# Cosine attention and a leaky-ReLU feed-forward: a planned stretch in the middle of the kernel replaced by an order written out by hand

## The chip, the cores and the metric

One NeuronCore of a Trainium2 chip runs the whole program. The metric is device time in microseconds (us) of one execution. The kernel before takes 428.02 us, the median of three runs (427.03 to 428.38).

The engines are named as the profile names them: PE (TensorE, matmuls; PEld are its weight loads), DVE (VectorE), ACT (ScalarE), POOL (GpSimd) and SP (SyncE, which here only issues DMAs). Each engine works through its own list of instructions in the order in which the program issued them; semaphores make one engine wait for another.

## The reference, cut to what matters

```python
# attention: 8 batches, 12 heads, 448 positions, 64 wide
q_n = q / (norm(q) + 1e-06);  k_n = k / (norm(k) + 1e-06)
scores = q_n @ k_n.T / tau                      # tau = 0.1
attn = exp(scores - max) / (sum(...) + 1e-09)
x = (attn @ v), heads side by side              # 3584 tokens, 768 wide
# feed-forward
h = x @ w_in                                    # 768 -> 2048
out = maximum(0.01 * h, h) @ w_out              # 2048 -> 768
```

Since the scores are cosines divided by 0.1, the kernel leaves the maximum out and takes the exponential at once.

## The kernel before, in words

**Tiles.** The work is cut in 48 slots. Slots 0 to 11 (batches 0 and 1) each hold q and k of one pair of heads. From slot 12 on (`OLD`, line 118) an even slot holds q and the next odd slot k of two pairs at once; such two slots are a unit, and slots 12 and 13 are unit 0. An attention group j is two pairs of heads; groups 3, 4 and 5 are those of batch 1 (slots 6 and 7, 8 and 9, 10 and 11). The tokens are cut in 8 chunks for the feed-forward; chunk 0 is the first 384 tokens of batch 0, chunk 1 the 512 tokens after them (the rest of batch 0 and all of batch 1).

**What a slot goes through**, with the engine and the line:

- `load_qk` (line 128): the load, issued by SP (lines 136, 144 to 147) into one of four buffers. A load waits until `normalise` and `squares` of the slot four before are done with the buffer.
- `squares` (195): POOL multiplies the raw tile by itself (lines 201, 208). `hold` (585) is a one-element copy on POOL that makes POOL wait for a `normalise` before its next squares.
- `sums` (210): DVE adds up the squares (216, 222). `roots` (226): two small ACT instructions that turn the sums into norms (229, 230).
- `normalise` (234): three or four DVE instructions, the last of which writes the normalised bf16 tile (238, 239, 245 or 255).
- `transposes` (283): up to slot 11 seven PE transposes (269) and a DVE copy (310); from slot 12 on a DVE transpose (291) and, for odd slots, six DMAs issued by SP that lay out the tiles of the unit (300).

**Attention.** `scores` and `key_tiles` (317, 320) and, for units, `quad_tiles` (391) multiply keys with queries into two PSUM banks per tile; ACT takes the exponentials (340, 408). `attend` (681) is one group of batch 1: `totals` (358: 16 matmuls, then two ACT instructions, 362 and 363, which give the reciprocal of the sums), two `products` (368) into two banks, and two `scale` (377: DVE, line 382), which write the attended tile `xT` and free the two banks. Two slots' tiles of batch 1, ki = 3, come as one tile with the odd slot.

**Feed-forward.** `first` (470) is 6 matmuls (line 476) and one ACT instruction (485); `second` (503) is 16 matmuls (line 507) and one DVE copy (518), and at its second half an output DMA on SP (527). Chunk 0 has 16 of the first and 6 of the second: 22 feed-forward groups. `feed_groups` (546) issues the next ones. The weights of `second` come in two halves by `load_w_out` (111), issued by POOL; the second half, which the last three groups of chunk 0 use, is asked for shortly before the stretch that is changed.

**PSUM.** `banks` (78) deals out the eight banks, always the pair or the single one whose last dealing is oldest. Which bank an instruction gets, and so whom it waits for, follows from the order in which the program asks.

**What sets the order.** Batch 0 and the first half of batch 1 are written out by hand (lines 619 to 745), up to the 13th feed-forward group of chunk 0, `normalise(10)` and `squares(11)`. Behind it stands a plan: the table `opened` (752) of five stretches with the attention group and the score tiles of each, and a loop (763) that hands out eight of the nine groups of chunk 0 that are left, by weights (`ATTEND`, `BLOCK`). In each stretch the slot `ahead` goes through `sums`, `roots`, `normalise`, `transposes`, the load of the slot two on, `hold` and the `squares` of the next slot. In the loop's stretches 2 and 3 `attend` stands first, then the scores, `sums`, `roots`, the feed-forward and only then the slot's `prepare`; the DVE instructions of `scale` get their inputs late and stand in DVE's list behind whatever the program issued between. Lines 800 to 803 then issue the load of slot 18, `sums(15)`, `squares(16)` and `roots(15)`.

From line 808 on a second plan lists the visits: three quad tiles in each, the products of the groups, and as many feed-forward groups as the level of the remaining work gives. Its visit 0 begins with `normalise(15)`, makes one quad tile, then `attend(5)` (`NEWQ - 1`), two more quad tiles and the one group of chunk 0 that was held back (`held`, 836). A weight of 3000 in `side` (831) stands for that `attend`. Chunk 1's groups begin behind visit 1's quad tiles.

## Time and profile before

| what | value |
|---|---|
| median of the runs | 428.02 us (427.03 to 428.38) |
| the profiled execution, its own time | 429.49 us |
| its span, first to last instruction | 427.7 us |
| what lies around the span | 1.8 us |
| busy: PE, ACT, DVE, POOL | 412.0, 255.2, 222.3, 116.7 us |
| mean granted TensorE clock | 0.992 |

The profile is one execution. Its views are: the page (busy times, the span in 40 slices with the granted clock, the costliest groups of instructions), the stretches (busy time of each engine between two times), the waits (who waited for whom), the chain of waits that ended last, and the timeline (instructions in order of time, merged; in brackets the idle time of the engine just before, and what ended it). A row such as `L402 PE MATMUL ps<-qkT` is line 402 on PE, writing `ps` from `qkT`; `xN` merges N instructions. Times of rows are from the span's start.

### The profile page before, as it was taken

To read this page: it belongs to the slowest core of one execution; us is meant where nothing else is said; L and a number is where in the kernel's file an instruction comes from. 1 tells how busy PE (TensorE), PEld (TensorE's weight loads), DVE (VectorE), ACT (ScalarE), POOL (GpSimd) and SP (SyncE) were. 2 spreads that over 40 slices of the span, in tenths; PEclk is the share of its full clock that TensorE was granted. 3 is DMA by queue.
4 is the path that set the end of the run, shared out by engine and by line. 5 is a ranking of instruction groups with operands and counts; after the bars stand their busy time and mean duration, and the time that the engine had idled before them with its cause. 6 is when DMAs were issued, how large, how long until landed. Compare 5 with 4: busy or idle time off the path is not lost.

```text
span 427.7 us, 11313 instructions
## 1 busy us (share of the span) xinstructions
PE 412.0 (96%) x4779; PEld 213.0 (50%) x4797; DVE 222.3 (52%) x385; ACT 255.2 (60%) x430; POOL 116.7 (27%) x149
## 2 busy tenths in 40 slices
PE   7899999879999999999999999999999999999996
PEld 2334544434455555554445555554445555654463
DVE  5887867564577755756673884366521312120021
ACT  3986866457866678657883868647674444104300
POOL 3875651353233323323430433033110000000000
PEclk9999999969999999999999999999999999999999
DMA  6999998676376862774374494643441200020021
GB/s 153 188 228 225 223 226 127 162 193 166 89 150 178 186 169 75 190 169 122 90 173 132 95 234 124 130 116 127 88 87 38 77 37 4 22 87 3 2 74 74
DMA packets 41907, 53.82 MB, mean 126 GB/s; under 512 B 12545, under 2 KB 32257, under 8 KB 41857
## 3 DMA queue, kind: packets, MB, share of 16 engines
q1 hardware_dynamic: 25680, 40.88, 34.3%
q0 software_dynamic: 15488, 11.80, 19.0%
q8 instruction: 37, 0.61, 0.6%
q10 hardware_dynamic: 688, 0.43, 0.4%
q14 instruction: 14, 0.11, 0.1%
HBM read 45.61 MB, written 11.01 MB: 132 GB/s over the span
## 4 chain that ended last, share of the span: by engine, by line
PE 85%; DMA 5%; DVE 4%; ACT 2%; SPq 1%; issue 1%; POOL 1%; ACTq 0%; POOLq 0%; DVEq 0%
PE ps L507 34%; PE ps L476 31%; PE ps L427 9%; PE ps L402 7%; DMA qk_h<-in_q_dram 3%; DMA qk_h<-in_k_dram 2%; DVE qn L255 1%; PE ps L351 1%; PE ps L331 1%; SPq L300 1%; PE ps L269 1%; PE ps L578 1%; ACT pe L340 1%; DVE qn L245 1%; DVE qkT L310 0%
## 5 line engine op out<-in xcount | busy, mean ns | idle before, releaser
L507 PE MATMUL ps<-w_out_sb,hT 128*128 128x384 bf16 x896 | 154.0, 330 | 1.2 <-DVE xT L382 1.2
L476 PE MATMUL ps<-xT,w_in_sb 128*128 128x384 bf16 (+1 forms) x753 | 149.8, 352 | 0.9 <-issue 0.2
L408 ACT ACTIVATE pe<-ps 128x896 bf16<-128x896 f32 x126 | 109.0, 916 | 43.5 <-PE ps L402 43.5
L507 PEld LDWEIGHTS <-hT 128*128 128x128 bf16 x896 | 86.2, 99 | 67.6 <-issue 14.2
L476 PEld LDWEIGHTS <-w_in_sb 128*128 128x128 bf16 x768 | 73.1, 98 | 73.5 <-issue 8.4
L485 ACT ACTIVATE hT<-ps 128x384 bf16<-128x384 f32 (+1 forms) x128 | 68.1, 548 | 62.8 <-PE ps L476 62.3
L518 DVE COPY osb<-ps 128x384 f32<-128x384 f32 (+1 forms) x56 | 30.9, 552 | 111.9 <-PE ps L507 106.2
L201 POOL TENSOR_TENSOR sq<-qk_h 128x896 f32<-128x896 f32 x36 | 61.2, 1701 | 6.2 <-DMA qk_h<-in_k_dram 5.0
L587 POOL CAST seen<-qn 128x1 f32<-128x1 bf16 x46 | 8.4, 184 | 174.2 <-DVE qn L245 168.0
L245 DVE TENSOR_TENSOR qn<-qk_h,r 128x896 bf16<-128x896 f32 x36 | 42.6, 1183 | 1.2
L402 PE MATMUL ps<-qkT 64*32 64x448 bf16 x1008 | 37.1, 354 | 3.5 <-ACT pe L408 3.5
L216 DVE TENSOR_REDUCE ss<-sq 128x14 f32<-128x896 f32 x36 | 37.5, 1042 | 4.0 <-POOL sq L201 4.0
L340 ACT ACTIVATE pe<-ps 128x896 bf16<-128x896 f32 x42 | 35.9, 917 | 5.7 <-PE ps L331 5.7
L238 DVE TENSOR_REDUCE r<-norms 128x14 f32<-128x28 f32 x48 | 8.6, 179 | 46.6 <-ACT norms L230 46.2
L291 DVE STREAM_TRANSPOSE tt<-qn 128x448 f32<-128x448 f32 x36 | 29.5, 820 | 0.9
L452 DVE TENSOR_TENSOR xT<-ps,rb 128x448 bf16<-128x448 f32 x32 | 18.4, 618 | 21.9 <-PE ps L427 20.8
L229 ACT ACTIVATE ss<-ss,tiny 128x14 f32<-128x14 f32 x48 | 14.6, 305 | 22.4 <-DVE ss L216 18.1
L427 PE MATMUL ps<-pe,vq 64*32 64x448 bf16 x1008 | 27.0, 349 | 0.0
L208 POOL TENSOR_TENSOR sq<-qk_h 128x384 f32<-128x384 f32 (+1 forms) x21 | 20.8, 1005 | 16.3 <-DMA qk_h<-in_k_dram 16.2
L402 PEld LDWEIGHTS <-qkT 64*32 64x32 bf16 x1008 | 13.1, 91 | 23.9 <-issue 18.8
L427 PEld LDWEIGHTS <-vq 64*32 64x32 bf16 x1008 | 14.5, 92 | 8.0 <-issue 0.3
L255 DVE TENSOR_TENSOR qn<-qk_h,r 128x512 bf16<-128x512 f32 (+1 forms) x24 | 17.0, 748 | 0.4
(52 smaller groups left out, 215.5 us busy)
## 6 DMA issues: line engine op xcount, KB each, us to landing
qk_h<-in_q_dram SPq DMA_DIRECT2D x36, 224.0 KB, 4.6
qk_h<-in_k_dram SPq DMA_DIRECT2D x36, 224.0 KB, 4.2
out_dram<-osb SPq DMA_DIRECT2D x20, 384.0 KB, 2.6
qkT<-tt SPq DMA_DIRECT2D x72, 56.0 KB, 2.1
qkT<-tt SPq DMA_DIRECT2D x36, 112.0 KB, 2.4
vq<-in_v_dram POOLq DMA_DIRECT2D x16, 224.0 KB, 4.8
w_in_sb<-in_moe_w_in_dram POOLq DMA_DIRECT2D x4, 768.0 KB, 10.4
w_out_sb<-in_moe_w_out_dram POOLq DMA_DIRECT2D x2, 1536.0 KB, 21.1
```

What stands on the lines that cost most here:

```text
L201: gp.tensor_tensor(sq, raw[s], raw[s], op=ALU.mult)
L216: nc.vector.tensor_reduce(ss[s], sqs[s].rearrange("p (t d) -> p t d", d=D), axis=AX.X, op=ALU.add)
L245: nc.vector.tensor_tensor(qn[s].rearrange("p m d e -> p m e d"), raw[s].rearrange(f"p ({t[1:-1]} d) -> p m e d", e=n, d=D), r.rearrange(f" ...
L291: nc.vector.transpose(out=to.rearrange(("p g (c m) -> p m g c", "p g (m c) -> p m g c")[which], m=7), in_=qn[s].bitcast(F32).rearrange("p ...
L340: nc.scalar.activation(out=dst, in_=sc[:, :, :S], func=AF.Exp, scale=inv_tau)
L402: nc.tensor.matmul(out=sc[32 * strip : 32 * strip + 32, a, :S], lhsT=x[rows, c0 : c0 + 32], rhs=x[rows, 0:S], start=True, stop=True,)
L408: nc.scalar.activation(out=pq[u, i], in_=sc[:, :, :S], func=AF.Exp, scale=inv_tau)
L427: nc.tensor.matmul(out=po[32 * strip : 32 * strip + 32, w, :S], lhsT=weights, rhs=pq[us[x if two else 0], i][rows, a, :], start=(i == 0), ...
L476: nc.tensor.matmul(out=pm[:, :n], lhsT=w_in_sb[:, kt, m * 128 : (m + 1) * 128], rhs=xT[c // 2][:, kt, c0 : c0 + n], start=(kt == 0), stop= ...
L485: nc.scalar.activation(out=hT[c][:, m, :n], in_=pm[:, :n], func=AF.Prelu, alpha=0.01)
L507: nc.tensor.matmul(out=po2[:, :HALF], lhsT=hT[c][:, m, ts * 128 : (ts + 1) * 128], rhs=w_out_sb[:, m, half * HALF : (half + 1) * HALF], st ...
L518: nc.vector.tensor_copy(out=o[:, half * HALF : half * HALF + cut], in_=po2[:, :cut])
```

## The change

The planned stretches and the three lines of constants go. In their place stands one order, written out, with the same operations. What differs:

- The loads of slots 15 and 16 stand ahead of unit 0's six tile DMAs (line 300, issued with slot 13) in SP's list; before they stood behind them. Squares go two slots ahead of `normalise` (`settle`), not one.
- `sums` and `roots` of slots 13, 14 and 15 stand one stretch ahead of the `normalise` that uses them; `roots(15)` stands before `attend(5)`.
- `attend(3)` and `attend(4)`, with their `scale`, stand ahead of `normalise(12)` and `normalise(13)` in DVE's list; before they stood behind them. Score tiles 10 and 11 of the third stretch come ahead of `attend(4)`.
- `transposes(10)` has a feed-forward group ahead of it; its copy and the eviction of that group come ahead of `sums(11)`.
- All nine groups that are left of chunk 0 are issued here. Visit 0 has its `attend(5)` ahead of it, prepares slot 15 before its three quad tiles, and then issues four groups of chunk 1. Since nothing is held back any more, the second plan shifts some feed-forward groups between later visits: whole groups move by a visit, and at the end the last visit has ten groups of `first` where it had six.

```diff
@@ -41,8 +41,6 @@
-    ATTEND = 5500
-    BLOCK = 1800
@@ -743,64 +741,66 @@
     hold(qn[s + 4][:, 6, 0, 0:1])
     squares(s + 5)
-    feed_groups(0, 1)
-    opened = [
-        (None, [(2, 0), (2, 1), (2, 2)], 5),
-        (None, [(3, 0), (3, 1), (3, 2)], 6),
-        (0, [(4, 0), (4, 1), (3, 3)], 7),
-        (1, [(4, 2), (5, 0), (5, 1)], 8),
-        (None, [(5, 2), (5, 3)], None),
-    ]
-    queue = []
-    b = 1
-    queue += work[0]
-    costs = [BLOCK + (ATTEND if at is not None else 0) for at, _, _ in opened[1:] + [(2, 0, 0)]]
-    for i, (at, tiles, ahead) in enumerate(opened):
-        share = (sum(g[0] for g in queue[:-1]) + sum(costs[i:])) / (len(opened) - i) - costs[i]
-        if at is not None:
-            attend(b * NQ + at)
-        if i == 0:
-            load_v(b * NQ + 2)
-        key_tiles([(b * NPAIR + p, ki) for p, ki in tiles])
-        done = 0
-        s = b * NPAIR + ahead if ahead else NSLOT
-        sums(s)
-        roots(s)
-        if i < 2:
-            if i == 1:
-                cost, fn = queue.pop(0)
-                fn()
-                done += cost
-            transposes(NPAIR + 4 + i)
-
-        def prepare():
-            normalise(s)
-            if s >= OLD:
-                transposes(s)
-            for n in ((s + 2,), (s + 2, s + 3))[i == 3]:
-                load_qk(n)
-            hold(qn[s][:, 6, 0, 0:1])
-            squares(s + 1)
-
-        if i < 2:
-            prepare()
-        while len(queue) > 1 and (i == len(opened) - 1 or done + queue[0][0] / 2 <= share):
-            cost, fn = queue.pop(0)
-            fn()
-            done += cost
-        if i in (2, 3):
-            prepare()
-        if i == 3:
-            load_vq(0)
-    load_qk(OLD + 6)
-    sums(OLD + 3)
-    squares(OLD + 4)
-    roots(OLD + 3)
+    load_v(s // 2 + 2)
+    load_qk(s + 7)
+    squares(s + 6)
+    feed_groups(0, 1)
+    def settle(s):
+        normalise(s)
+        if s >= OLD:
+            transposes(s)
+        hold(qn[s][:, 6, 0, 0:1])
+        squares(s + 2)
+
+    scores(s + 2, (0, 1, 2))
+    feed_groups(0, 1)
+    transposes(s + 4)
+    sums(s + 5)
+    feed_groups(0, 2)
+    roots(s + 5)
+
+    scores(s + 3, (0, 1, 2))
+    load_qk(s + 8)
+    settle(s + 5)
+    feed_groups(0, 1)
+    sums(s + 6)
+    roots(s + 6)
+    transposes(s + 5)
+    attend(NQ)
+
+    scores(s + 4, (0, 1))
+    scores(s + 3, (3,))
+    load_qk(s + 9)
+    settle(s + 6)
+    sums(s + 7)
+    feed_groups(0, 1)
+    roots(s + 7)
+
+    scores(s + 4, (2,))
+    scores(s + 5, (0, 1))
+    feed_groups(0, 1)
+    attend(NQ + 1)
+    load_qk(s + 10)
+    settle(s + 7)
+    sums(s + 8)
+
+    scores(s + 5, (2, 3))
+    feed_groups(0, 1)
+    load_vq(0)
+    roots(s + 8)
+    load_qk(s + 11)
+    settle(s + 8)
+    load_qk(s + 12)
+    sums(s + 9)
+    feed_groups(0, 1)
+    roots(s + 9)
+    attend(NEWQ - 1)
+    feed_groups(0, 1)
@@ -829,16 +829,16 @@
     side = [
-        3000 if n == 0 else 0 if n not in parts or parts[n][1] is None else 7 * S
+        0 if n not in parts or parts[n][1] is None else 7 * S
         for n in range(len(visits))
     ]
-    held = [(False, g) for g in queue]
+    held = []
...
-        scaling = n == 0 or e is not None
+        scaling = e is not None
@@ -852,8 +852,6 @@
         quad_tiles(tiles[:1])
-        if n == 0:
-            attend(NEWQ - 1)
```

In the new code s is 6, so `s + 9` is slot 15.

## The prediction

> **What bounds the kernel now.** I read the page first, then the busy times by stretches, then PE's waits, then the timeline around the longest wait.

> ```profile
> PE 412.0 (96%) x4779; PEld 213.0 (50%) x4797; DVE 222.3 (52%) x385; ACT 255.2 (60%) x430; POOL 116.7 (27%) x149
> ```

> ```profile
> 58.00:95.00 37.00, 32.19 (x348) 16.20 (x348) 24.66 (x43) 19.58 (x36) 13.67 (x15) 0.91 0.85 173
> 95.00:370.00 275.00, 274.35 (x3687) 144.02 (x3699) 146.68 (x235) 182.62 (x301) 65.88 (x80) 1.00 0.48 119
> 370.00:427.70 57.70, 53.98 (x300) 29.26 (x299) 7.22 (x14) 9.87 (x17) 0.00 (x0) 1.00 0.14 48
> ```

> Behind the length stand the busy us of PE, PEld, DVE, ACT and POOL, then granted clock, DMA share and GB/s. PE bounds the kernel: from 95 to 370 us it idles 0.65 us, so there is nothing to win there, only to lose. In 58 to 95, the stretch that the change rewrites, it idles 4.8 us and its clock is 0.91. Who makes it wait:

> ```profile
> PE ps L402 <- ACT pe L408: 3.5, 1, 3.5
> PE ps L507 <- DVE xT L382: 1.2, 2, 0.8
> ```

> The timeline around the wait of 3.5 us:

> ```profile
> 75.45 3.77 SPq L300 DMA_DIRECT2D qkT<-tt  x6
> 79.34 1.16 SPq L136 DMA_DIRECT2D qk_h<-in_k_dram  x2
> 84.09 1.68 POOL L201 TENSOR_TENSOR sq<-qk_h 128x896 f32<-128x896 f32 x1 [2.98 <-DMA qk_h<-in_k_dram]
> 85.81 1.09 DVE L216 TENSOR_REDUCE ss<-sq 128x14 f32<-128x896 f32 x1 [3.37 <-POOL sq L201]
> 86.93 0.31 ACT L229 ACTIVATE ss<-ss,tiny 128x14 f32<-128x14 f32 x1 [6.20 <-DVE ss L216]
> 87.39 0.90 ACT L408 ACTIVATE pe<-ps 128x896 bf16<-128x896 f32 x1
> 88.34 0.57 PE L402 MATMUL ps<-qkT 64*32 64x448 bf16 x8 [3.48 <-ACT pe L408]
> 88.84 5.30 PE L507 MATMUL ps<-w_out_sb,hT 128*128 128x384 bf16 x16
> 94.07 0.79 PE L402 MATMUL ps<-qkT 64*32 64x448 bf16 x24
> ```

> It is one chain. SP issues the load of slot 15 only behind the six tile DMAs of unit 0, so the load starts at 79.3 and the squares at 84.1. The sums and roots follow; `roots(15)` stands in ACT's list ahead of visit 0's first exponential, which therefore starts at 87.4 although its matmuls were long done; and PE's third quad tile waits for that exponential's bank. Then 16 matmuls take 5.30 us. Why:

> ```profile
> 86.00:88.00 2.00, 0.00 (x0) 0.00 (x0) 1.32 (x3) 1.04 (x3) 0.97 (x2) 0.84 1.02 272
> 93.00:94.00 1.00, 1.00 (x4) 0.28 (x2) 0.00 (x0) 0.00 (x0) 0.00 (x0) 0.50 0.77 161
> 94.00:95.00 1.00, 0.86 (x25) 0.37 (x26) 0.78 (x3) 0.43 (x1) 0.00 (x0) 0.91 0.35 84
> ```

> The clock is granted at a half: a mean of 0.84 over 86 to 88 means the fall came near 87.4, some 2.5 us after PE stopped (88.34 less 3.48 is 84.86); 0.91 over 94 to 95 puts its return at 94.2.

> **The change part by part.** First PE's own list, to the end of visit 0's three quad tiles, where everything that the old program had done before its quad tiles of 94.07 is done too. Durations, start to start where two rows follow each other:

> ```profile
> 55.64 0.81 PE L269 MATMUL ps<-id,qn 128*128 128x128 bf16 x7 [0.89 <-DVE qn L255]
> 56.29 3.09 PE L476 MATMUL ps<-xT,w_in_sb 128*128 128x384 bf16 x18
> 61.91 0.76 PE L331 MATMUL ps<-qkT 64*64 64x448 bf16 x12
> 62.60 2.77 PE L507 MATMUL ps<-w_out_sb,hT 128*128 128x384 bf16 x16
> 69.65 2.76 PE L507 MATMUL ps<-w_out_sb,hT 128*128 128x384 bf16 x16 [0.81 <-DVE xT L382]
> 72.34 0.75 PE L351 MATMUL ps<-pe,ones 128*32 128x448 bf16 x12
> 74.73 0.76 PE L331 MATMUL ps<-qkT 64*64 64x448 bf16 x12
> ```

> A `first` group is a third of 3.09, 1.03; twelve score matmuls are 0.69 (61.91 to 62.60); a `second` group is 2.69 (69.65 to 72.34), an `attend` 2.39 (72.34 to 74.73), seven transposes about 0.6. The transposes of slot 10 end at 56.29 in both orders, since their source sets that; the change puts one `first` group into the 0.89 us in front of them. From 56.29 PE has left: two `first` 2.06, six `second` 16.14, three `attend` 7.17, score matmuls 12+12+12+8 2.53, transposes 0.6, 24 quad matmuls 0.69 (as the scores): 29.2 us, so 85.5 against 94.07, if nothing waits. These 8.6 us are the 1.0 of the moved group, the 3.48, the 0.81 and the rest of the 1.2, and 5.30 less 2.77, 2.5, for the clock, with some 0.4 of hand-overs.

> What is late next? DVE and ACT hand work to and fro, and there the new order is a chain.

> ```profile
> L216 DVE TENSOR_REDUCE ss<-sq 128x14 f32<-128x896 f32 x5 | 5.4, 1078 | 4.0 <-POOL sq L201 4.0
> L382 DVE TENSOR_TENSOR xT<-ps,rb 128x448 bf16<-128x448 f32 x6 | 3.4, 609 | 0.2 <-ACT rb L363 0.2
> L518 DVE COPY osb<-ps 128x384 f32<-128x384 f32 x6 | 3.3, 558 | 6.8 <-PE ps L507 6.8
> L291 DVE STREAM_TRANSPOSE tt<-qn 128x448 f32<-128x448 f32 x4 | 3.3, 818 | 0.1
> ```

> ```profile
> 73.34 0.54 ACT L362 ACTIVATE rb<-ps 128x448 f32<-128x448 f32 x1 [1.56 <-PE ps L351]
> 73.91 0.58 ACT L363 ACTIVATE rb<-rb 128x448 f32<-128x448 f32 x1
> 87.51 0.18 DVE L238 TENSOR_REDUCE r<-norms 128x14 f32<-128x28 f32 x1 [0.62 <-ACT norms L230]
> 88.00 1.17 DVE L245 TENSOR_TENSOR qn<-qk_h,r 128x896 bf16<-128x896 f32 x1
> ```

> Prices: `scale` twice 0.61, 1.22; `normalise` 1.66 (87.51 to 89.17), DVE transpose 0.82, sums 1.08, so 3.6 with hand-overs for "a slot"; roots 0.46 (86.93 to 87.39); the two logarithm instructions of `totals` 1.15 (73.34 to 74.49); an exponential 0.9. Now in the new lists. The first `second` group ends on PE at 61.7; its eviction 0.56, `sums(12)` 1.08 and `roots(12)` 0.46 lead to 63.9, the logarithms of `attend(3)` to 65.0, `scale(3)` to 66.3. The bank that the next `second` group gets comes from its first half, at 65.7, against PE at 65.4: a wait of 0.3 is left of the 0.81, because `scale` no longer stands behind `normalise(12)` and its transpose. On: slot 12 with `sums(13)` 69.9; `roots(13)` 70.4; three exponentials, which stand behind these roots on ACT, 73.1; logarithms 74.3; `scale(4)` 75.5; slot 13 with `sums(14)` 79.1; roots with an eviction beside them 79.7; slot 14 with `sums(15)` 83.3; `roots(15)` 83.8; logarithms of `attend(5)` 85.0; `scale(5)` 86.2, say 86.4 with hand-overs. The bank dealing gives the third quad tile of visit 0 the two banks of `attend(5)`, so PE, there at 85.6, waits 0.8 and the quad tiles end at 86.6. Squares are no part of this: the load of slot 15 now goes out when slot 11's buffer is free, near 61, and POOL has each square done a stretch before its sum.

> Next the transfers that move. The loads of 15 and 16 used to start at 79.3 and later; now they start near 61 and, behind `normalise(12)`, near 68. There the DMA queues were moving the second half of `w_out`:

> ```profile
> 53.95 1.16 POOL L113 DMA_DIRECT2D w_out_sb<-in_moe_w_out_dram  x1
> ```

> ```profile
> w_out_sb<-in_moe_w_out_dram POOLq DMA_DIRECT2D x1, 1536.0 KB, 17.5
> ...
> qkT<-tt SPq DMA_DIRECT2D x8, 56.0 KB, 2.0
> ```

> ```profile
> 69.00:70.00 1.00, 0.35 (x3) 0.21 (x3) 1.00 (x3) 1.00 (x2) 1.00 (x1) 1.00 1.40 196
> ```

> The last column of the DMA rows is the median time to landing. `w_out` landed at 53.95 plus 17.5, 71.5; the new order wants it on PE for the fourth `second` group at 74.7. The two loads are 2 x 448 KB; at the row's 196 GB/s 4.7 us. If they go wholly ahead of `w_out`, it lands at 76.2 and PE waits 1.5; if not at all, nothing. I take the first, the end that the row is nearer to, a saturated engine share (1.40). PE would then reach the third quad tile after the bank is free: the two waits don't add up, and the quad tiles end at 87.3.

> [...]

> Sum: 94.07 less 86.6 to 87.3 is 6.8 to 7.5. I take 6.9, near the `w_out` case. The profiled execution, 429.49 (span 427.7 and 1.8 around it), would become 422.6; it lies 1.5 above the median, and on the median's footing the forecast is 428.02 less 6.9, **421.1**.

> Edits at no cost, and their cover. Unit 0's tiles leave DVE near 78 and need 3.77 us on SP and about 2 to land, 83.9; their reader comes at 85: cover 1. Unit 1's tiles: `normalise(15)` follows `scale(5)`, tile DMAs from 89.5 to 93.3, landed at 95.5; the reader is the second tile of visit 2, behind two times four groups of chunk 1:

> ```profile
> 95.02 5.13 PE L476 MATMUL ps<-xT,w_in_sb 128*128 128x512 bf16 x23 [0.16 <-issue]
> ```

> 87 plus 2 x 5.35 plus 1.0 is 98.7: cover 3. The shifted groups of later visits are the same matmuls; where a chunk starts, a `second` group (2.69) less now lies between `scale` and its reader, and the last visit's end has three `first` groups less behind the last products, where chunk 6's six `second` groups remain as cover for their `scale`. I cost these at nothing, down to the 0.65 us that could be won there and up to 1 us lost.

> **The rivals.**

> *R1, the stall moves.* The DVE and ACT chain runs through `scale(5)`. If it is over 1.7 us longer than summed, the third quad tile waits more than 2.5 us and the clock falls again, another 2.5 to 2.7. For it: roots still stand in front of exponentials on ACT, now `roots(13)`, and in front of logarithms, `roots(15)`. Against: DVE was busy 24.7 of 37 us. End at 88.3 plus 2.7, 91.0: 3.1 gained, 424.9.

> [...]

> *R2, absorbed later.* PE comes 7 us earlier to the visits; slots 15 to 17 or the loads do not keep up, and it waits there. Against: a cover of 3 at unit 1. If half is given back: 424.5.

> *R3, slower: `w_out`.* If the second half lands at X, PE idles X less 74.7 and the clock falls. The quad tiles then end at 85.8 plus that plus 2.7; this equals 94.07 from X = 80.3, 8.8 us later than now. Against: the added 917 KB would have to pass at 104 GB/s. For it: 196 GB/s was the sum of all queues, and the row does not show how they share it. At X = 82: 429.7.

> *R4, it doesn't do what it says.* The load of 15 still waits, for its buffer or another queue, and the same stall stands at another place: 428.0. Against: in SP's list it now stands ahead of everything that waited.

> **How the numbers follow.** Forecast (gain 5.5 to 8.6) 0.70; R1 0.12; R2 0.09; R3 0.05; R4 0.04. The range reaches from PE alone, 8.6 gained (419.4), to R1 at 424.9; outside lie R3, R4 and the tail of R2. About 0.3%, 1.3 us, is what a measurement of this kernel can tell from no change. Faster by more than that: forecast, R1 and most of R2, 0.90; within it R4, 0.04; slower R3 and what is unseen, 0.06.

> **What would show it.** The profile after should have no wait of PE on line 408 over 1 us and a clock of 1.00 throughout; the squares of slot 15 should not wait for their load; `scale(3)` and `scale(4)` should stand ahead of the slots' `normalise`; a wait of PE at line 507 for a DMA near 75 would show `w_out`; a wait at line 402 for line 382 near 86 the chain. Chunk 1's first group should start near 87 where it started at 94.8. The forecast is wrong if PE idles over 2.5 us at one place, or if 95 to 370 loses more than 1 us.

## The result, and the profile after

| | before | after |
|---|---|---|
| median | 427.91 us (4 runs) | 421.27 us (4 runs, 421.03 to 421.61) |
| ratio | | 0.9848, 95% interval 0.983 to 0.9865 |
| profiled execution, its span | 429.49, 427.7 us | 421.03, 419.2 us |
| mean granted clock of it | 0.992 | 1.000 |

The change takes 6.6 us off the median; the forecast was 6.9. Over all the runs of this study before has a median of 428.27 (37 runs beside the experiments) and after one of 421.5 (12 runs, 421.03 to 422.37). Lines of the code after stand two lower than before: 402 is 400, 507 is 505, 382 is 380.

The page of after, PE's busy time; then its stretches, with the columns as in the prediction; then all that PE waits for:

```profile
PE 410.0 (98%) x4797; PEld 211.9 (51%) x4797; DVE 223.0 (53%) x385; ACT 254.4 (61%) x430; POOL 116.6 (28%) x149
```

```profile
58.00:95.00 37.00, 36.62 (x381) 18.51 (x381) 27.31 (x44) 23.86 (x42) 14.67 (x16) 1.00 0.92 196
95.00:370.00 275.00, 275.00 (x3713) 145.34 (x3712) 145.37 (x234) 176.76 (x292) 64.23 (x78) 1.00 0.48 117
```

```profile
PE ps L576 <- DVE pe L559: 1.6, 1, 1.6
PE ps L267 <- DVE qn L253: 1.0, 1, 1.0
PE ps L329 <- ACT pe L338: 0.8, 3, 0.3
PE ps L329 <- ACT norms L228: 0.8, 1, 0.8
PE ps L329 <- DVE qkT L308: 0.6, 2, 0.3
PE ps L505 <- DVE xT L380: 0.4, 1, 0.4
```

PE's idle time between 58 and 95 us has fallen from 4.8 to 0.4 us, and the clock there has risen from 0.91 to 1.00. The wait of 3.5 us at the quad tiles has no row any more. The one row left in the changed stretch is the last, 0.4 us for a `scale`. The work that is the same in both, from chunk 1's first group to the end, takes the same time: 419.2 less 85.5 (below) is 333.7 us, and before 427.7 less 94.8, plus the 0.7 us of the quad tiles that stood ahead of it there, is 333.6. The whole gain lies ahead of that point.

The timeline of after, by engines: SP first, then the slot of the long wait through POOL, DVE and ACT, then PE.

```profile
61.67 1.54 SPq L134 DMA_DIRECT2D qk_h<-in_k_dram  x2
67.57 1.10 SPq L134 DMA_DIRECT2D qk_h<-in_q_dram  x2
77.26 4.17 SPq L298 DMA_DIRECT2D qkT<-tt  x6
...
76.64 1.68 POOL L199 TENSOR_TENSOR sq<-qk_h 128x896 f32<-128x896 f32 x1
...
81.27 1.04 DVE L214 TENSOR_REDUCE ss<-sq 128x14 f32<-128x896 f32 x1
82.22 0.55 DVE L516 COPY osb<-ps 128x384 f32<-128x384 f32 x1
83.97 1.16 DVE L380 TENSOR_TENSOR xT<-ps,rb 128x448 bf16<-128x448 f32 x2 [1.20 <-ACT rb L361]
...
82.34 0.31 ACT L227 ACTIVATE ss<-ss,tiny 128x14 f32<-128x14 f32 x1 [3.67 <-DVE ss L214]
82.80 0.53 ACT L360 ACTIVATE rb<-ps 128x448 f32<-128x448 f32 x1
...
65.46 2.76 PE L505 MATMUL ps<-w_out_sb,hT 128*128 128x384 bf16 x16 [0.38 <-DVE xT L380]
74.44 5.37 PE L505 MATMUL ps<-w_out_sb,hT 128*128 128x384 bf16 x32
84.83 0.76 PE L400 MATMUL ps<-qkT 64*32 64x448 bf16 x24
85.53 4.71 PE L474 MATMUL ps<-xT,w_in_sb 128*128 128x512 bf16 x21
```

The load of slot 15 (the first row) goes out at 61.7 instead of 79.3, ahead of the six tile DMAs. Its squares (76.64) no longer wait for it, and its sums (81.27) stand in their turn on DVE. ACT still waits 3.67 us for those sums, with `roots(15)` at the head of its list, but now PE has nothing that needs ACT in that time. The 24 quad matmuls run in one piece at 84.8, before they were in three, and chunk 1 begins at 85.5.

The second half of `w_out` in the DMA view of after (issued at 53.69; last column the time to landing):

```profile
w_out_sb<-in_moe_w_out_dram POOLq DMA_DIRECT2D x1, 1536.0 KB, 20.7
```

It lands at 74.4, and PE takes it up at 74.44: no wait of the matmuls, and no cover left. The weight load in front of them does wait for it; PEld's row in the waits between 58 and 95 us:

```profile
PEld L505 <- DMA w_out_sb<-in_moe_w_out_dram: 0.4, 1, 0.4
```

### The profile page after: what moved, and what is told of

Read it like the earlier page. It is cut to its first block, busy times and chain, and to the rows that moved or that the text cites. A ratio compares the mean times of both kernels' runs of the same rounds, so it can differ in the third digit from the quotient of the medians.

```text
span 419.2 us, 11328 instructions
## 1 busy us (share of the span) xinstructions
PE 410.0 (98%) x4797; PEld 211.9 (51%) x4797; DVE 223.0 (53%) x385; ACT 254.4 (61%) x430; POOL 116.6 (28%) x149
## 4 chain that ended last, share of the span: by engine, by line
PE 89%; DMA 3%; DVE 3%; ACT 3%; issue 0%; SPq 0%; DVEq 0%
PE ps L505 35%; PE ps L474 33%; PE ps L425 9%; PE ps L400 7%; PE ps L349 3%; DMA qk_h<-in_q_dram 3%; DVE qn L253 2%; ACT pe L338 1%; PE ps L329 1%; PE ps L576 1%; DMA qk_h<-in_k_dram 1%; PE ps L267 1%; ACT ss L227 0%; ACT hT L483 0%; ACT norms L228 0%
## 5 line engine op out<-in xcount | busy, mean ns | idle before, releaser
L505 PE MATMUL ps<-w_out_sb,hT 128*128 128x384 bf16 x896 | 151.3, 326 | 0.4 <-DVE xT L380 0.4
L505 PEld LDWEIGHTS <-hT 128*128 128x128 bf16 x896 | 85.5, 98 | 65.2 <-issue 10.3
L253 DVE TENSOR_TENSOR qn<-qk_h,r 128x512 bf16<-128x512 f32 (+1 forms) x24 | 18.2, 798 | 0.4
## 6 DMA issues: line engine op xcount, KB each, us to landing
w_out_sb<-in_moe_w_out_dram POOLq DMA_DIRECT2D x2, 1536.0 KB, 22.6
```

Source lines behind the costliest of these rows:

```text
L505: nc.tensor.matmul(out=po2[:, :HALF], lhsT=hT[c][:, m, ts * 128 : (ts + 1) * 128], rhs=w_out_sb[:, m, half * HALF : (half + 1) * HALF], st ...
```

## The experiments

The theory: SP's order was the cause; the load that stood behind the tile DMAs held back sums, roots and, by ACT's order, the exponential, and PE's idle time dropped its clock. The rivals: the place of roots and attention groups carries the gain and the load is hidden; the slow matmuls have another cause than the idle time.

**1. Before, with the load of slot 15 ahead of the tile DMAs.**

```diff
         def prepare():
+            for n in ((s + 2,), (s + 2, s + 3))[i == 3]:
+                load_qk(n)
             normalise(s)
             if s >= OLD:
                 transposes(s)
-            for n in ((s + 2,), (s + 2, s + 3))[i == 3]:
-                load_qk(n)
```

> The kernel before with one edit: in the stretch's prepare the loads are issued ahead of normalise and the transposed tiles, so the load of slot 15 stands ahead of unit 0's six tile DMAs on SP. Theory (the load's place is the cause of the long wait): squares(15) then start behind hold(14), near 81, sums(15) end near 83.9, roots(15) near 84.5, the first quad exponential at 85.4; PE waits about 0.6 instead of 3.5 and the clock stays at 1.00: about 5.6 us less, 422.4 (up to 424 if the clock's share is smaller in the median run than in the profiled one). Rival (what counts is that the attention groups and roots stand elsewhere; the load is hidden anyway): less than 1 us off 428.

Measured: 423.55 us (4 runs) against 428.28, ratio 0.9897 (0.9869 to 0.9924). PE's waits and timeline of this run:

```profile
PE ps L507 <- DVE xT L382: 1.2, 2, 0.8
...
PE ps L402 <- ACT pe L408: 0.5, 1, 0.5
```

```profile
85.11 0.38 PE L402 MATMUL ps<-qkT 64*32 64x448 bf16 x8 [0.46 <-ACT pe L408]
85.42 2.77 PE L507 MATMUL ps<-w_out_sb,hT 128*128 128x384 bf16 x16
```

The long wait shrinks to 0.46, and the group behind it is back at 2.77 us. This one edit of SP's order gives 4.7 of the 6.8 us between the medians of all runs. The waits for `scale` (1.2) stay, as they should. The other parts of the new order, with the load ahead, give the 2.0 that are left (423.55 to 421.5).

**2. After, with the loads of 15 and 16 behind the tile DMAs.**

```diff
-    load_qk(s + 9)
-    settle(s + 6)
+    normalise(s + 6)
+    transposes(s + 6)
+    hold(qn[s + 6][:, 6, 0, 0:1])
+    squares(s + 8)
...
+    normalise(s + 7)
+    transposes(s + 7)
+    load_qk(s + 9)
     load_qk(s + 10)
-    settle(s + 7)
+    hold(qn[s + 7][:, 6, 0, 0:1])
+    squares(s + 9)
```

(The two `settle` are written out; only the place of the two loads changes.)

> The kernel after with one edit: the loads of slots 15 and 16 are issued behind unit 0's six tile DMAs, as before the change; all else as after. Theory: the tile DMAs end on SP near 81.4, the load of 15 lands near 86, squares near 88, sums(15) 89, roots(15) 89.5, then the logarithms and scale of attend(5) near 92; PE's third quad tile waits for that scale from 85.3, some 6 us, and the clock falls for another 2.5: about 8 us more than after, 429 to 430, slower than the kernel before. Rival (the other parts of the order carry the gain): within 1 us of 421.3.

Measured: 430.72 us (6 runs), ratio to before 1.0063 (1.0041 to 1.0085): slower than before, and 9.2 more than after. PE's waits, DVE's timeline, and the stretches behind them:

```profile
PE ps L400 <- DVE osb L516: 4.2, 1, 4.2
...
PE ps L400 <- DVE xT L380: 1.2, 1, 1.2
```

```profile
88.20 1.09 DVE L214 TENSOR_REDUCE ss<-sq 128x14 f32<-128x896 f32 x1 [6.37 <-POOL sq L199]
89.20 0.55 DVE L516 COPY osb<-ps 128x384 f32<-128x384 f32 x1
```

```profile
86.00:88.00 2.00, 0.00 (x0) 0.00 (x0) 0.00 (x0) 0.00 (x0) 1.51 (x1) 0.91 0.95 261
...
96.00:98.00 2.00, 2.00 (x6) 0.76 (x5) 0.00 (x0) 0.04 (x2) 0.08 (x1) 0.53 0.56 134
```

The sign and nearly the size were expected, the place not quite: PE already waits at the second quad tile, 4.2 us, for a bank whose eviction stands behind `sums(15)` on DVE, and then 1.2 for `scale(5)`. The clock is at a half from about 87.6 (0.91 of two us) to 97.9 (0.53 of two us), 10.2 us. The rest of the new order, without the loads, is worth less than nothing: an eviction that PE needs now stands behind `sums(15)` too, PE's two waits make 5.4 us instead of 3.5, and the half clock lasts longer. So the two parts of the change do not simply add up.

**3. Before, with matmuls in the place of the wait.** The added 14 matmuls write a bank that nobody reads.

```diff
-        quad_tiles(tiles[1:])
+        if n == 0:
+            quad_tiles(tiles[1:2])
+            wm = banks(1)
+            for i in range(14):
+                nc.tensor.matmul(out=wm, lhsT=w_in_sb[:, 0, 0:128], rhs=w_in_sb[:, 0, 0:512], ...)
+            quad_tiles(tiles[2:])
+        else:
+            quad_tiles(tiles[1:])
```

> The kernel before with 14 matmuls of 128x512, whose result nobody reads, put on PE between visit 0's second and third quad tile, where it waits 3.5 us; 14 take about 3.0 us at full clock, so nothing that is needed comes later. Theory (the 16 slow matmuls behind the wait are the price of PE's idle time, by the clock): the clock stays at 1.00, the second group behind takes 2.8 instead of 5.3: 2.5 us less, about 425.4. Rival (they are slow for another reason, contention with the loads that land then): 428, or up to 0.5 more.

Measured: 426.93 us (10 runs), ratio 0.9961 (0.9942 to 0.998). The timeline of the run:

```profile
84.64 3.19 PE L869 MATMUL ps<-w_in_sb 128*128 128x512 bf16 x14
87.76 0.38 PE L402 MATMUL ps<-qkT 64*32 64x448 bf16 x8
88.12 2.76 PE L507 MATMUL ps<-w_out_sb,hT 128*128 128x384 bf16 x16
```

Useless work on PE makes the kernel faster: the group behind takes 2.76 instead of 5.30 us, in the presence of the same loads (285 GB/s over 88 to 90 us, in before 316). And it is not one lucky execution: all 10 have a mean clock of 0.998 or more, where only 4 of the 37 of before have 0.999 and the other 33 have 0.996 or less. So it was the idle time. But the gain is 1.35 us at the median, not 2.5.

**4. Before once more.**

> The kernel before once more, for a second profile of it. Theory: the same wait of 3.3 to 3.7 us for slot 15 and a half clock behind it; the profiled execution of before lay 1.5 us above the median, so the time at half clock may differ from 6.8 us. Rival (the wait is an accident of one execution): another wait, or none.

Measured: 428.41 us, mean clock 0.996 instead of 0.992. Its stretches and the group behind the wait:

```profile
88.00:90.00 2.00, 1.48 (x12) 0.59 (x12) 1.78 (x3) 1.97 (x4) 0.48 (x1) 0.58 1.10 324
90.00:92.00 2.00, 2.00 (x9) 1.00 (x8) 2.00 (x4) 1.12 (x2) 1.87 (x3) 0.57 0.95 194
```

```profile
88.52 0.57 PE L402 MATMUL ps<-qkT 64*32 64x448 bf16 x8 [3.19 <-ACT pe L408]
89.02 4.08 PE L507 MATMUL ps<-w_out_sb,hT 128*128 128x384 bf16 x16
```

The same wait, 3.19, but half clock for 3.4 us only (at 0.50, where the rows of before and of experiment 2 have it for whole us, a mean of 0.58 over two us is 1.7 us at a half, and the next row as much), where the first profile had 6.8, and 4.08 us for the group instead of 5.30. So the first profile promised experiment 3 more than most executions had to give. The 37 executions of before that ran beside the experiments fall into three groups by their mean granted clock: 0.999 and more, 4 executions, median 426.8 us; 0.995 or 0.996, 26, median 428.0; 0.992, 7, median 430.0. The first group is where experiment 3 lies, 426.93. The profile that the prediction was made from belongs to the last.

**5. After, with the two scales behind `normalise`.**

```diff
-    attend(NQ)
+    attend(NQ, False)                 # no scale here
...
     settle(s + 6)
+    scale(NQ, 0)
+    scale(NQ, 1)
```

and the same for `attend(NQ + 1)` and `settle(s + 7)`.

> The kernel after with one edit: the scale of attend(3) and of attend(4) is issued behind normalise and the DVE transpose of slots 12 and 13, as before the change. Theory: scale(3) then begins near 66.5 instead of 64.8, and the second group whose bank it frees waits some 2.0 us instead of 0.4 at 65; scale(4) is late too but nobody waits for it. PE is 1.6 us later from there on, and reaches the third quad tile after scale(5) is done: 1.6 us more than after, 422.9. Rival (only what the kernel before shows at these waits, 1.2 in all, comes back): 0.8 more. Second rival (the chain through scale(5) now ends last): 3 us or more.

Measured: 423.69 us (4 runs), against 422.08 of after in the same set (experiment 8). PE's waits and DVE's timeline:

```profile
PE ps L505 <- DVE xT L380: 1.8, 1, 1.8
```

```profile
67.47 1.13 DVE L380 TENSOR_TENSOR xT<-ps,rb 128x448 bf16<-128x448 f32 x2
```

One wait of 1.8 us for `scale(3)` against 0.4; 1.6 us more at the median. The theory's size holds, and the second late scale costs PE nothing, as it said.

**6. After, with the second half of `w_out` asked for later.**

```diff
-    load_w_out(1)
     sums(s + 3)
...
     settle(s + 6)
+    load_w_out(1)
```

> The kernel after with one edit: the second half of w_out is asked for behind the squares of slot 14, near 69.5 instead of 53.7. In the profile after it landed at 74.4, when PE took it up at 74.4. Theory (the rival of the prediction that ended slower, its price): at 196 GB/s and more it lands near 78.5, PE waits 4 us, and the half clock behind the wait adds 0 to 2.9 us, by execution: 425.3 to 428.2, median near 426.8. Rival (there is cover left behind the landing): under 1 us more than after.

Measured: 430.03 us (10 runs), ratio to before 1.0046 (1.0032 to 1.006). The DMA view and PE's timeline:

```profile
w_out_sb<-in_moe_w_out_dram POOLq DMA_DIRECT2D x1, 1536.0 KB, 11.4
```

```profile
81.33 7.54 PE L505 MATMUL ps<-w_out_sb,hT 128*128 128x384 bf16 x32 [6.29 <-DMA w_out_sb<-in_moe_w_out_dram]
```

It needs 11.4 us, not the 9 that I had reckoned, so PE waits 6.3, and the two groups behind take 7.54 instead of 5.37, in an execution with a mean clock of 0.991 (after's is 1.000). The mechanism of the rival that ended slower is real, and there is no cover behind the landing.

**7. After, with the logarithms of `attend(3)` ahead of `roots(12)`,** a try at the 0.4 us that is left; **8,** the kernel after beside it; **10 and 11,** both kernels once more.

```diff
-    roots(s + 6)
     transposes(s + 5)
     attend(NQ)
+    roots(s + 6)
```

> The kernel after with one edit: roots(12) is issued behind attend(3), so the logarithms of attend(3) do not stand behind roots(12), and so behind sums(12), on ACT. Theory: they start near 63.0 instead of 63.6, scale(3) at 64.2, and the last wait of this stretch on PE, 0.4 us, goes: 420.9, in the profile a PE without a wait at the line of the second groups. Rival (normalise(12) is pushed back by the later roots and with it the chain through scale(5)): 421.3 or up to 1 us more.

> The kernel after once more, beside the other three on the same chip: 421.3, spread under 1 us, since its clock does not fall; the rival, that it falls in some executions as in the kernel before, would show as executions 1 to 3 us longer.

> The kernel with roots(12) behind attend(3) once more, in five rounds beside after, to tell 0.3 us apart: theory 0.3 to 0.5 us under after; the profile before this showed the 0.4 us wait gone and a new one of 0.3 us for the second half of w_out, so the rival is no difference.

> The kernel after once more beside these two: 421.3 to 422.1, the medians of its two earlier sets.

Measured: 420.98 (4 runs, 420.76 to 421.42) beside after's 422.08 (4, 421.12 to 422.3); again 421.75 (5, 420.67 to 423.18) beside 421.65 (4, 421.33 to 422.37). The timelines of the two profiles of the edit:

```profile
74.19 5.37 PE L505 MATMUL ps<-w_out_sb,hT 128*128 128x384 bf16 x32 [0.32 <-DMA w_out_sb<-in_moe_w_out_dram]
```

```profile
76.58 5.37 PE L505 MATMUL ps<-w_out_sb,hT 128*128 128x384 bf16 x32 [1.22 <-DMA w_out_sb<-in_moe_w_out_dram]
```

The wait for `scale(3)` is gone in both, and PE now waits for `w_out`, 0.3 and 1.2 us: in the first PE came 0.6 us earlier than in after, in the second `w_out` was asked for 1.2 us later (54.90 instead of 53.69) and took 21.6 us. Whether the edit gains anything stays open; the two sets disagree.

After itself, expected at 421.3 with a spread under 1 us, came out at 422.08 with a spread of 1.2 in experiment 8. Its clock stayed at 0.999 or more, so the clock is not the reason. 0.5 us of it are there ahead of the changed order, whose first score matmuls begin at 54.09 instead of 53.55: before them PE waits 1.6 us instead of 1.0 for normalised tiles (line 267).

**9. After, with `transposes(10)` ahead of the group.**

```diff
-    feed_groups(0, 1)
     transposes(s + 4)
+    feed_groups(0, 1)
     sums(s + 5)
```

> The kernel after with one edit: transposes(10) is issued ahead of the first of the feed-forward groups behind scores(8), as before the change, not behind it. Theory: PE waits for the normalised slot 10 as in the kernel before, 0.9 us, and the group comes on top: 0.9 to 1.0 more than after, 422.2 to 422.5. Rival (the group's place costs nothing, since the stretch behind is set by the chain over DVE and ACT): within 0.3 of after.

Measured: 422.43 us (4 runs) against 421.65 of after in the same set. PE's timeline has the old wait back:

```profile
55.92 0.81 PE L267 MATMUL ps<-id,qn 128*128 128x128 bf16 x7 [0.90 <-DVE qn L253]
```

0.8 us more, near the 0.9 to 1.0 expected, though within what two medians of four runs leave open.

## Why the prediction was right, and what in it was wrong

- **The cause of the long wait**: right, by experiments 1 and 2. The load's place alone gives most of the gain, and taking it back alone costs more than the gain.
- **The moved group and the scales**: right. 0.3 us was forecast to be left of the wait for `scale(3)`; 0.38 was. Experiment 5 puts 1.6 us on the scales' place in the new order, experiment 9 0.8 on the group's, though that is within what its few runs leave open.
- **The `w_out` term, 1.5 us**: mis-sized. The two loads moved its landing by 3.2 us (17.5 to 20.7; 20.9 and 20.7 in the two further profiles of after), not 4.7, and it landed when PE came for it. That the loads did it, the experiments show: with both loads behind the tile DMAs (experiment 2) it took 17.4, with the load of slot 15 alone ahead (experiment 1) 18.9. The step that failed took the whole of the loads as going ahead of it. The wait itself is real: 0.2 us show in the profile of experiment 8 (the score matmuls of 74.47 end near 74.98, PE goes on at 75.18, and its weight load waits 0.6 for `w_out`), 0.3 in experiment 7, where PE comes a little earlier, and 6.3 in experiment 6.
- **The chain through `scale(5)`**: forecast to end at 86.2 to 86.4, it ended at 85.13 (83.97 plus 1.16), and PE, there at about 85.3, had no wait for it. The parts, small each: the timeline of after already stands 0.26 earlier at the transposes of slot 10; the transpose of slot 13 is a k slot's and took 0.65 instead of the mean of 0.82 (74.80 to 78.09 for the slot, 3.3 instead of 3.6); three exponentials took 2.5, not 2.7. The quad tiles ended at 85.5, where "PE alone" had put them.
- **The clock's 2.5 us**: right for the profiled execution, wrong for the median. The two profiled executions differ by 8.46 us (429.49 to 421.03), the medians by 6.6. The step that failed is "on the median's footing": the sum was made from an execution with the longest time at half clock and then taken off the median as it was. At the median the clock's part is 1.2 (428.0 against 426.8 of the executions with a mean clock of 0.999 or more).
- So two errors of the sum work against each other: two new waits were forecast that did not come (1.5 of the 1.8 us between 85.5 and 87.3; the other 0.3, `scale(3)`'s, came), and the clock was counted with 1.3 too much for the median. With both set right the sum is 8.6 less 0.3 less 1.3, 7.0; the 0.2 to 0.4 us to the measured 6.8 (all runs) and 6.6 no run here assigns. That 6.9 comes so near to 6.6 is luck in part: the sum looks better than its terms.
- **Later visits**: at nothing, rightly; 333.6 against 333.7 us.
- **The rivals**: the stall did not move (R1), nothing was given back later (R2), and the load did what it was moved for (R4). R3's formula, at a landing of 81.3, gives 85.8 plus 6.6 plus 2.7, 95.1, 1.0 more than the 94.07 of before: 429.1; experiment 6 gave 430.03. In its profile the quad tiles end at 94.6, and that execution, 430.07, lies 0.6 above the profiled one of before; the rest of the difference is the step "on the median's footing" again, which R3 shares.

## What to carry to other kernels

Where what releases a long wait was itself waiting, follow the chain back, also through the queue that only issues transfers: here one load stood behind six DMAs that waited for a computation, and its place in SP's list was worth 4.7 us. Before a sum made from one profiled execution is taken off a median, look whether that execution is like the others; the mean granted clock of each run told it here, 0.992 where 26 of the 37 executions have 0.995 or 0.996. And when a reordering brings a transfer forward, look up who else is on the queues at that time: the second half of the weights took 20.7 us to land instead of 17.5 and lost all its cover, and PE's own rows of waits do not show it, only the 0.4 us of its weight load.

## What the runs showed of the hardware that was not expected

In 4 of the 37 executions the mean clock stayed at 0.999 or more with that wait in the program; why, no run shows, since those executions left no profile.
